# Three small copies on ScalarE in each of 24 dense units, and nine wide matmuls instead of twelve at the start

## The chip, the core and the metric

The kernel runs on one core of a Trainium2 chip. A core has five engines that run side by side, each with a list of instructions of its own: TensorE (PE in the profile, its weight loads PEld), VectorE (DVE), ScalarE (ACT), GpSimd (POOL) and SyncE (SP, which only issues transfers here). The metric is the device time of one execution in microseconds; the figure for the kernel before is a median of 3 runs.

## The reference

Three computations that share no data, in float32:

```
# 1 retention attention, 2 x 8 heads, 768 steps, width 64
for t in range(S):
    state = gamma * state + k[t] (x) v[t]          # 64 x 64 a head
    y[t] = scale * q[t] @ state
# 2 dense feed-forward, 1536 tokens, 512 -> 2048 -> 512
h = x @ w_in
out = maximum(0.01 * h, h) @ w_out
# 3 feed-forward with 8 experts, 512 -> 1024 -> 512
logits = x @ w_gate
e = argmax(logits); gate = softmax(logits)[e]
out[i] = gate[i] * (relu(x[i] @ w1[e]) @ w2[e])    # up to 384 tokens an expert
```

In this kernel they are chained: the attention's output is the input of the dense part, and that of the dense part the input of the experts.

## The kernel before

Weights and activations of the large matmuls are split into a high and a low part of reduced width, and each product is made as three (high x high, low x high, high x low); ScalarE makes a high part with one copy, VectorE the low part with one subtraction.

**The front.** The sequence runs as 12 chunks of 128 steps (named 0 to 9, a, b). The constant `LOADS` sets the order in which SP issues the loads (q0, k0, q1, w00 ...), and the constant `FRONT` sets the order of all steps of attention and of the first dense units, on all engines: `S.0` scores of chunk 0 (L190, PE), `am` the mask that multiplies them (L212, DVE), `M` scores times values (L256, PE), `ks` scaled keys (L198, DVE for the first two chunks, L202, ACT for the others), `D` the state's update (L228, PE), `Y` queries times state (L245, PE), and so on. Ahead of `S.0` PE runs matmuls on a tile of zeros whose results nobody reads: twelve wide ones (L1023, 512 columns) and one that clears the state (L217, `zero_state`); after `S.0` it runs 24 narrow ones (L1075, 64 columns), while VectorE makes the first masks.

**The dense part** is 64 units. A unit is 12 matmuls into `ps_h` (L363), then ScalarE copies them (`hs`, L370), VectorE applies the leaky maximum (L375), ScalarE rounds to the high part (`gh`, L379), VectorE makes the low part (`gl`, L385), and two units later (`LAG = 2`) PE multiplies by the second weight (L414, `ps_y`). Twelve units are begun in the front (the variable `reached` counts them, so it is 12), the loop that the diff touches runs over the others, i = 12 to 63. The function `slot()` in it puts the conversion of further weights between the steps (L297, L308 on ScalarE, L291 and others on VectorE).

**The experts** are 8, each with 8 units of weights. How many tokens an expert has is known only when the kernel runs, so the code of each is there three times, for 2, for 3 and for 1 tile of 128 tokens, in this order, and a comparison on every engine (L1231, L1232) jumps to the body that is run:

```
with tc.If(n > base + P, preferred_fallthrough_block=True, label=f"many{s}") as many:
    with tc.If(n <= base + 2 * P, preferred_fallthrough_block=True) as two:
        expert(s, 2, o)
    with two.Else():
        expert(s, 3, o)
with many.Else():
    expert(s, 1, o)
```

With this input the experts s = 0 to 7 run the bodies for 2, 3, 1, 1, 1, 1, 2 and 2 tiles. In a body, `mm_h` (L820 for one tile, L826 for two and three) makes h, `gh` (L868, ACT) and `gl` (L869, DVE) split it, `mm_y` (L878) makes y, and `og` (L982 on ACT, L980 on DVE) scales it by the gate. In the body for one tile all 8 h come first and then all 8 y. `conv_next` converts one unit of weights, ScalarE the high part `hi` (L848) and VectorE the low part `lo` (L849); behind an expert's own weights it takes up the first three units of the next expert, in the full width of 1024. It may do so only when the y whose buffer it takes has been made, so in a body for one tile these three stand behind the last `gh`, while PE is at the 8 y. The lines L747 and L750 are the comparisons of `by_class`, which choose between three ways to transpose the next expert's tokens, and L1302 a hint to the branch at the next expert.

## Time and profile before

| | |
|---|---|
| median of 3 runs | 533.26 us (532.6 to 534.32) |
| the profiled execution's own time | 533.35 us |
| its span in the trace | 531.6 us |
| mean granted clock of TensorE | 0.994 |
| busy share PE / PEld / DVE / ACT / POOL | 96% / 86% / 64% / 45% / 10% |

The span runs from the first to the last recorded work; the 1.75 us by which the execution's own time is longer lie around it. Busy shares are shares of the span. In the rows below, a line of a timeline gives the start, the time that the group took, the engine, the line of the program, the operation, what it writes and reads, how many there are, and in brackets how long the engine was idle just before and what ended that.

### The profile page before, as it was taken

What the parts mean: (1) busy time and instruction counts of PE and PEld (TensorE: products, weight loads), DVE (VectorE), ACT (ScalarE), POOL (GpSimd) and SP (SyncE); (2) the same over time, 40 slices, a digit from 0 to 9 for tenths busy, and PEclk for the clock granted to TensorE, in tenths of its full rate; (3) what the DMA queues carried; (4) which work ended last, traced back from release to release, by engine and by line L of the source; (5) the groups of instructions that cost most, each with busy time, mean ns of one, the idle gap of its engine ahead of it and who ended that gap; (6) DMA issues with size and microseconds to landing.
All of it is one profiled execution on the core that took longest, in us unless ns stands there. A gap on an engine that the chain in (4) does not pass through costs nothing.

```text
span 531.6 us, 8978 instructions
## 1 busy us (share of the span) xinstructions
PE 511.9 (96%) x3330; PEld 458.4 (86%) x3330; DVE 338.7 (64%) x670; ACT 241.0 (45%) x501; POOL 51.9 (10%) x75
## 2 busy tenths in 40 slices
PE   8899999999999999999999999999699989999994
PEld 5888989989998899988999998889599978889893
DVE  3999994379779748954733365667444445676560
ACT  1886963354344424432431314256243455556440
POOL 0000000000000000000100027242100211220101
PEclk9999999999999999999999999999989999999999
DMA  8987672022325602220210108599263298992001
GB/s 319 369 269 260 224 251 94 1 81 79 100 53 175 222 7 80 80 80 0 80 59 2 60 10 326 171 301 328 90 229 103 67 360 301 350 344 79 23 10 43
DMA packets 24939, 80.79 MB, mean 152 GB/s; under 512 B 3706, under 2 KB 3834, under 8 KB 24864
## 3 DMA queue, kind: packets, MB, share of 16 engines
q1 hardware_dynamic: 21312, 70.26, 37.8%
q0 software_dynamic: 3552, 9.58, 5.1%
q8 instruction: 40, 0.66, 0.5%
q14 instruction: 35, 0.29, 0.2%
HBM read 72.35 MB, written 9.96 MB: 155 GB/s over the span
## 4 chain that ended last, share of the span: by engine, by line
PE 72%; DMA 21%; DVE 3%; issue 1%; ACT 1%; POOL 0%; POOLq 0%; ACTq 0%; DVEq 0%
PE ps_h L363 24%; PE ps_y L414 16%; DMA out<-og,gix 12%; DMA xr<-x2d,gix 7%; PE ps_a L414 7%; PE ps_y L878 5%; PE ps_h L826 5%; PE ps_a L256 2%; PE ps_a L190 2%; PE ps_a L245 2%; PE ps_a L463 1%; PE ps_h L704 1%; DMA xpre<-wc,wix 1%; PE ps_y L715 1%; PE ps_y L1023 1%
## 5 line engine op out<-in xcount | busy, mean ns | idle before, releaser
L370 ACT ACTIVATE hs<-ps_h 128x384 f32<-128x384 f32 x64 | 31.5, 492 | 108.6 <-PE ps_h L363 108.6
L375 DVE SCALAR_TENSOR_TENSOR hs<-hs 128x384 f32<-128x384 f32 x64 | 35.6, 556 | 65.8 <-ACT hs L370 65.6
L414 PE MATMUL ps_y<-hi,gh 128*128 128x512 f32 x138 | 56.3, 408 | 0.0
L363 PE MATMUL ps_h<-xh,hi 128*128 128x384 f32 x256 | 55.8, 340 | 0.0
L363 PE MATMUL ps_h<-xh,lo 128*128 128x384 f32 x256 | 54.9, 336 | 0.0
L363 PE MATMUL ps_h<-xl,hi 128*128 128x384 f32 x256 | 54.8, 336 | 0.0
L414 PE MATMUL ps_y<-hi,gl 128*128 128x512 f32 x138 | 54.5, 395 | 0.0
L414 PE MATMUL ps_y<-lo,gh 128*128 128x512 f32 x138 | 54.4, 394 | 0.0
L379 ACT ACTIVATE gh<-hs 128x384 fp32r<-128x384 f32 x64 | 33.7, 526 | 43.5 <-DVE hs L375 43.5
L363 PEld LDWEIGHTS ps_h<-xh,hi 128*128 128x128 f32 x256 | 45.9, 188 | 5.3
L385 DVE TENSOR_TENSOR gl<-hs,gh 128x384 fp32r<-128x384 f32 x64 | 35.6, 557 | 21.3 <-ACT gh L379 21.3
L363 PEld LDWEIGHTS ps_h<-xl,hi 128*128 128x128 f32 x256 | 45.3, 188 | 0.0
L363 PEld LDWEIGHTS ps_h<-xh,lo 128*128 128x128 f32 x256 | 45.3, 188 | 0.0
L849 DVE TENSOR_TENSOR lo<-xland,hi 128x1024 fp32r<-128x1024 f32 (+1 forms) x32 | 33.6, 1056 | 14.0 <-ACT hi L848 13.4
L878 PE MATMUL ps_y<-hi,gh 128*128 128x512 f32 x104 | 41.2, 396 | 0.0
L878 PE MATMUL ps_y<-hi,gl 128*128 128x512 f32 x104 | 41.0, 394 | 0.0
L878 PE MATMUL ps_y<-lo,gh 128*128 128x512 f32 x104 | 40.8, 392 | 0.0
L849 DVE TENSOR_TENSOR lo<-land,hi 128x1024 fp32r<-128x1024 f32 (+1 forms) x30 | 31.2, 1044 | 10.3 <-ACT hi L848 9.9
L869 DVE SCALAR_TENSOR_TENSOR gl<-ps_h,gh 128x256 fp32r<-128x256 f32 (+2 forms) x42 | 16.6, 395 | 26.0 <-ACT gh L868 25.7
L848 ACT ACTIVATE hi<-xland 128x1024 fp32r<-128x1024 f32 (+1 forms) x32 | 29.2, 920 | 7.4 <-PE ps_y L878 7.4
L868 ACT ACTIVATE gh<-ps_h 128x256 fp32r<-128x256 f32 (+2 forms) x42 | 15.3, 363 | 38.0 <-PE ps_h L826 23.9
L414 PEld LDWEIGHTS ps_y<-hi,gl 128*128 128x128 f32 x138 | 25.9, 188 | 5.8
(200 smaller groups left out, 1000.0 us busy)
## 6 DMA issues: line engine op xcount, KB each, us to landing
land<-wc SPq DMA_DIRECT2D x32, 512.0 KB, 6.7
xland<-wc SPq DMA_DIRECT2D x32, 512.0 KB, 5.0
land<-wb SPq DMA_DIRECT2D x31, 512.0 KB, 4.9
land<-qkv SPq DMA_DIRECT2D x19, 512.0 KB, 5.4
out<-zero SPq DMA_DIRECT2D x12, 256.0 KB, 6.3
x2d<-rows SPq DMA_DIRECT2D x12, 256.0 KB, 2.1
early<-qkv SPq DMA_DIRECT2D x5, 512.0 KB, 7.0
cst<-cst_in SPq DMA_DIRECT2D x1, 512.0 KB, 5.5
```

The source lines that it names most:

```text
L363: nc.tensor.matmul(out=h_ps, lhsT=w[i][:, dc * P:(dc + 1) * P], rhs=x[j][:, dc, :], start=(n == 0), stop=(n == 3 * KD - 1))
L370: nc.scalar.activation(out=hs, in_=gt[u][0], func=ACTF.Copy)
L375: nc.vector.scalar_tensor_tensor(out=hs, in0=hs, scalar=0.01, in1=hs, op0=ALU.mult, op1=ALU.max)
L379: nc.scalar.activation(out=gh, in_=gt[u][0], func=ACTF.Copy)
L385: nc.vector.tensor_tensor(out=gl, in0=hs, in1=gh.bitcast(F32), op=ALU.subtract)
L414: nc.tensor.matmul(out=yb[ti][t], lhsT=gt[u][i][:, t * P:(t + 1) * P], rhs=w[j][:, 512:1024], start=(f == fs[0] and n == 0), stop=(f == fs ...
L826: r = nc.tensor.matmul(out=hp, lhsT=w[i][:, dc * P:(dc + 1) * P], rhs=(h, l)[j][:, dc, 0:cls * P], start=(n == 0), stop=(n == 3 * KD - 1))
L848: nc.scalar.activation(out=hi[:, o], in_=src[:, o], func=ACTF.Copy)
L849: nc.vector.tensor_tensor(out=lo[:, o], in0=src[:, o], in1=hi[:, o].bitcast(F32), op=ALU.subtract)
L868: nc.scalar.activation(out=gh, in_=hp, func=ACTF.Relu)
L869: nc.vector.scalar_tensor_tensor(out=gl, in0=hp, scalar=0.0, in1=gh.bitcast(F32), op0=ALU.max, op1=ALU.subtract)
L878: nc.tensor.matmul(out=yps[t], lhsT=gg[i][:, t * P:(t + 1) * P], rhs=w[j][:, 512:1024], start=(k == 0 and n == 0), stop=(k == PF - 1 and n ...
```

## The change

It has three parts. On TensorE three of the twelve wide matmuls on zeros go, and three narrow ones are added. On ScalarE each of the 24 units i = 12 to 35 of the dense loop gets three copies of one number into a tile `tick` that nothing reads. No other line is changed.

```diff
         nc.scalar.activation(out=bias_e, in_=zero[:, 0:1], func=ACTF.Copy)
+        tick = sm_p.tile([1, 1], F32, name="tick", bufs=1)
         wm = bank("y2", [P, DM])
-        for i in range(12):
+        for i in range(9):
             nc.tensor.matmul(out=wm, lhsT=zb[:, 0:P], rhs=zb[:, 0:DM], start=True, stop=True)
         zero_state(0)
...
             if n == "S" and c[0] == 0:
-                for _ in range(24):
+                for _ in range(27):
                     nc.tensor.matmul(out=wm[0:32, 0:64], lhsT=zb[:, 0:32], rhs=zb[:, 0:64], start=True, stop=True)
...
             slot()
             if i == len(units) - 1:
                 break
+            if i - reached < 24:
+                for _ in range(3):
+                    nc.scalar.activation(out=tick, in_=zero[0:1, 0:1], func=ACTF.Copy)
             u = units[i - LAG]
             ensure(u[1], 1)
```

On TensorE at the start of the program, before the change, the last wide matmuls on the tile `zero`, the state's clearing, the scores and the first narrow matmuls stand like this (a LDWEIGHTS row loads the weights of the matmul under it):

```order
L1023 LDWEIGHTS zero
L1023 MATMUL ps_y<-zero 128x512
L217 LDWEIGHTS zero
L217 MATMUL ps_h<-zero 128x512
L190 MATMUL ps_a<-early 128x128 x8
L1075 LDWEIGHTS zero
L1075 MATMUL ps_y<-zero 32x64
```

And with the change (the line numbers grow by one):

```order
L1024 LDWEIGHTS zero
L1024 MATMUL ps_y<-zero 128x512
L217 LDWEIGHTS zero
L217 MATMUL ps_h<-zero 128x512
L190 MATMUL ps_a<-early 128x128 x8
L1076 LDWEIGHTS zero
L1076 MATMUL ps_y<-zero 32x64
```

The order is the same; ahead of the first piece nine pairs stand instead of twelve, so everything from L217 on is six instructions earlier, and behind the narrow ones the counts are equal again.

On ScalarE in the dense loop, before the change, one unit follows the other like this (`hs` and `gh` are a unit's copies, `cv_a` and `hi` the conversion of a further weight, `rows` a finished output):

```order
L424 ACTIVATE rows<-ps_y 128x512 x3
L370 ACTIVATE hs<-ps_h 128x384
L379 ACTIVATE gh<-hs 128x384
L297 ACTIVATE cv_a<-cv_a,bias_e 128x512 x2
L370 ACTIVATE hs<-ps_h 128x384
L379 ACTIVATE gh<-hs 128x384
L308 ACTIVATE hi<-cv_a 128x512 x2
```

And with the change, over the same units:

```order
L424 ACTIVATE rows<-ps_y 128x512 x3
L370 ACTIVATE hs<-ps_h 128x384
L379 ACTIVATE gh<-hs 128x384
L297 ACTIVATE cv_a<-cv_a,bias_e 128x512 x2
L1144 ACTIVATE tick<-zero 1x1 x3
L370 ACTIVATE hs<-ps_h 128x384
L379 ACTIVATE gh<-hs 128x384
L308 ACTIVATE hi<-cv_a 128x512 x2
L1144 ACTIVATE tick<-zero 1x1 x3
```

The three copies stand in front of the next unit's `hs`, behind `gh` or behind the conversion of a weight; nothing else changes places.

On ScalarE at the end of the body for one tile of expert s = 2, before the change, after the comparisons about the transposes, stand the last `gh`, the three conversions for the next expert, the scaled output and the jump out of the body:

```order
L785 ACTIVATE cxf<-ps_a 128x256
L750 UNCONDITIONAL_BRANCH
L868 ACTIVATE gh<-ps_y 128x128
L848 ACTIVATE hi<-xland 128x1024
L747 UNCONDITIONAL_BRANCH
L848 ACTIVATE hi<-xland 128x1024 x2
L982 ACTIVATE og<-ps_y,tab 128x512
L1231 UNCONDITIONAL_BRANCH
```

And with the change:

```order
L785 ACTIVATE cxf<-ps_a 128x256
L750 UNCONDITIONAL_BRANCH
L868 ACTIVATE gh<-ps_y 128x128
L848 ACTIVATE hi<-xland 128x1024
L747 UNCONDITIONAL_BRANCH
L848 ACTIVATE hi<-xland 128x1024 x2
L982 ACTIVATE og<-ps_y,tab 128x512
L1235 UNCONDITIONAL_BRANCH
```

The rows are the same but for the line number. What moves is their place in ScalarE's list: 72 instructions are added ahead of them, and 26 semaphore instructions fall away there (the built program has 372 on ScalarE before and 346 with the change), because a wait that had an instruction of its own now rides on a copy. So every body of an expert on ScalarE stands 46 instructions later. The lists of the other engines keep their length and order, but for the three matmuls above.

## Rows read from the trace of the kernel before

**Rows 1.** The page, part 1: TensorE's busy time, share of the span, instructions.

```profile
PE 511.9 (96%) x3330; PEld 458.4 (86%) x3330; DVE 338.7 (64%) x670; ACT 241.0 (45%) x501; POOL 51.9 (10%) x75
```

**Rows 2.** The chain of waits, 355 to 532 us: who waited for whom, total, times, longest.

```profile
PE ps_y L820 <- DVE lo L849: 2.7, 3, 1.1
...
PE ps_h L820 <- DVE lo L849: 1.1, 1, 1.1
```

**Rows 3.** Timeline of TensorE, ScalarE and VectorE, end of s = 2 and start of s = 3.

```profile
428.09 0.48 PE L878 MATMUL ps_y<-hi,gh 128*128 128x512 f32 x1
...
433.70 1.05 PE L820 MATMUL ps_h<-cxf,xland 128*128 128x128 f32 x8
435.83 1.16 PE L820 MATMUL ps_h<-cxf,xland 128*128 128x128 f32 x8 [1.08 <-DVE lo L849]
438.11 2.05 PE L820 MATMUL ps_y<-cxf,xland 128*128 128x128 f32 x16 [1.11 <-DVE lo L849]
...
428.60 0.27 ACT L868 ACTIVATE gh<-ps_y 128x128 fp32r<-128x128 f32 x1
433.46 2.95 ACT L848 ACTIVATE hi<-xland 128x1024 fp32r<-128x1024 f32 x3 [4.60 <-PE ps_y L878]
...
434.56 3.50 DVE L849 TENSOR_TENSOR lo<-xland,hi 128x1024 fp32r<-128x1024 f32 x3 [5.14 <-ACT hi L848]
437.97 0.29 DVE L869 SCALAR_TENSOR_TENSOR gl<-ps_h,gh 128x128 fp32r<-128x128 f32 x1
```

**Rows 4.** Timeline of ScalarE, the same place in s = 3, 4 and 5.

```profile
448.97 2.00 ACT L848 ACTIVATE hi<-land 128x1024 fp32r<-128x1024 f32 x2 [3.01 <-PE ps_y L878]
...
462.87 2.01 ACT L848 ACTIVATE hi<-xland 128x1024 fp32r<-128x1024 f32 x2 [2.52 <-PE ps_y L878]
...
478.95 1.06 ACT L848 ACTIVATE hi<-land 128x1024 fp32r<-128x1024 f32 x1 [3.33 <-PE ps_h L826]
```

**Rows 5.** The transfers of 431 to 433.6 us: instruction fetches (packets, MB, share).

```profile
q14 instruction: 1, 0.01, 0.7%
```

**Rows 6.** Timeline of TensorE and VectorE, the start of the program.

```profile
1.19 5.30 PE L1023 MATMUL ps_y<-zero 128*128 128x512 bf16 x12 [1.19 <-DVE zero L1019]
6.28 0.63 PE L217 MATMUL ps_h<-zero 128*128 128x512 bf16 x1
6.84 1.16 PE L190 MATMUL ps_a<-early 64*128 64x128 f32 x16
7.94 0.87 PE L1075 MATMUL ps_y<-zero 128*32 128x64 bf16 x24
...
9.38 0.98 PE L256 MATMUL ps_a<-am,early 128*64 128x128 f32 x13 [0.17 <-DVE am L212]
...
8.04 1.29 DVE L212 TENSOR_TENSOR am<-ps_a,cst 128x512 f32<-128x512 f32 x2 [6.91 <-PE ps_a L190]
```

**Rows 7.** Timeline of SP: the loads that it issues, each behind an earlier landing.

```profile
5.31 1.66 SPq L164 DMA_DIRECT2D land<-qkv  x2
...
8.69 0.33 SPq L164 DMA_DIRECT2D land<-qkv  x1
```

**Rows 8.** Windows: busy time of each engine, PEclk (granted clock), DMA share, GB/s.

```profile
385.00:389.10 4.10, 4.04 (x14) 4.07 (x15) 0.00 (x0) 0.30 (x1) 0.00 (x0) 0.58 0.02 6
```

**Rows 9.** ScalarE: the smallest copy, `hs` in 100 to 200 us (busy, mean | idle), and one tight unit.

```profile
2.03 0.20 ACT L1020 ACTIVATE bias_e<-zero 128x1 f32<-128x1 f32 x1
...
L370 ACT ACTIVATE hs<-ps_h 128x384 f32<-128x384 f32 x24 | 11.8, 491 | 38.4 <-PE ps_h L363 38.4
...
121.82 0.49 ACT L370 ACTIVATE hs<-ps_h 128x384 f32<-128x384 f32 x1 [0.71 <-PE ps_h L363]
```

**Rows 10.** Timeline of ScalarE, VectorE and TensorE in the body of s = 1.

```profile
410.68 1.05 ACT L848 ACTIVATE hi<-land 128x1024 fp32r<-128x1024 f32 x1
...
415.02 0.56 DVE L869 SCALAR_TENSOR_TENSOR gl<-ps_h,gh 128x384 fp32r<-128x384 f32 x1 [2.03 <-ACT gh L868]
...
418.48 0.39 PE L878 MATMUL ps_y<-hi,gh 128*128 128x512 f32 x1
```

## The prediction, made before the changed kernel ran

> **What bounds the kernel now.** I read the page first: TensorE is busy 96% of the span [rows 1], so time can only be won where it stands idle, or where its matmuls run at the lower clock. The chain of waits, then, for the experts: what ends TensorE's idle time there, beside one branch, is VectorE's `lo`, 2.7 us in three pieces and 1.1 us in one [rows 2], 3.8 us in all. In the dense part TensorE's timeline shows no idle stretch. So three places matter: those four pieces, the start, and the dense units for the cover that they give.

> [...]

> **The change part by part.**

> *Bodies 46 places later.* The copies add 72 instructions ahead of the experts and 26 semaphore instructions go. Borders then lie 46 places earlier in the code than now. I followed each through the bodies that this input runs: the four in the bodies for one tile fall into code for three tiles, which isn't run there, and one enters run code, in s = 1. Without a stop the first conversion of s = 2 starts at about 429.05. The first `lo` started 1.10 us after its conversion (434.56 less 433.46), and the three took 3.50: they end at 429.05 + 1.10 + 3.50 = 433.65. TensorE wants them after its first eight matmuls of s = 3, at 433.70 + 1.05 = 434.75. So they are 1.1 us early, and so, by the same shape, in the other three. The four pieces go whole: minus 3.8 us. What is late next is nothing on these rows: TensorE itself.

> *The border in s = 1.* It falls beside the conversion at 410.68, ahead of the last `gh` [rows 10]. With the longest stop seen, the conversion starts at 415.3 and ends at 416.3, `gh` takes some 0.5 and its `gl` starts near 416.9, ending at 417.5 (0.56 us). TensorE reads that at 418.48. So about 1 us of cover is left; a stop over 5.6 us would show. Bound 0 to 0.3; I take 0.1.

> *Nine wide matmuls.* Twelve and what follows start 6.28 - 1.19 = 5.09 us apart, 0.424 each, so three are 1.27 us [rows 6]. The scores could start at 6.84 - 1.27 = 5.57; SP's row at 5.31, which stands behind the landing of the first load, says that their data is there by then [rows 7]. [...] The 16 scores of 128 columns, 6.84 to 7.94, are 0.069 apart, a quarter of 0.234 and a little: full pace. [...] Gain 0.65. [...] Behind the scores the mask follows 0.04 us on [rows 6], and everything in `FRONT` hangs on that chain. The scaled keys need a constant that lands at 8.67 (SP goes on at 8.69, [rows 7]) and wouldn't start 0.65 earlier than their 9.24, but 0.55; `D`, which wants them, follows the M matmuls at about 9.55, and the keys end near 9.4. I take 0.65 of 0 to 1.27.

> *Three more narrow matmuls.* 0.87 / 24 is 0.036 each, so 0.11 us, ahead of M; M waits 0.17 us for the second mask two matmuls later (9.38), which takes it up [rows 6]. Cost 0; without that cover 0.11.

> *The 72 copies.* The smallest copy in the rows, 128 by 1, takes 0.20 us; three make 0.6 us a unit. They stand ahead of `hs`, where ScalarE idles for TensorE's h anyway: 38.4 us over 24 units between 100 and 200 us, 1.6 us each [rows 9]. A tight unit has 0.71. Where the cover fails `hs` is later by some tenths, and behind it VectorE's leaky maximum, `gh` and `gl`; TensorE reads them two units on, four blocks of matmuls of about 2 us, against a chain of some 3.5. So 0; uncovered everywhere it would be 24 x 0.6 = 14 us. Lower bound 0: nothing waits for the copies.

> **The sum.** 533.35 (the profiled execution) - 3.8 - 0.65 + 0.1 = 529.0. That execution lies 0.09 above the median of the runs, so the sum holds for a median as well. Its own range: from 533.35 - 3.8 - 1.27 = 528.3, less 0.4 for runs, to 530.3, where the start gives nothing and a fifth of the stops stays: 527.9 to 530.3.

> **The rivals.**

> 1. *The start gives nothing or costs.* After the branch into s = 1 the rows show a stretch of 4.1 us at a granted clock of 0.58 behind TensorE's idle time [rows 8]: low pace can last some us. [...] Chance 0.12.

> 2. *The stops move instead of going.* The jumps into the bodies for one tile now lead from one block into the next, which they don't today on ScalarE. If such a jump misses, `gh` at the start of the next expert is late and the conversions behind it with it. VectorE makes a jump of this kind between s = 2 and s = 3 now, and its row at 437.97 shows no idle time behind the `lo` before it [rows 3], which speaks against. With half to all of the 3.8 given back: 530.9 to 532.7. Chance 0.16, about half of it under the 531.7 that can be told from no change. [...]

> 3. *A border costs nothing,* the regular distance is an accident, and `lo` stays late for a transfer or for y. Then only the start counts: 532.7. Against it: the wandering place. Chance 0.06.

> 4. *Slower: the copies stand in TensorE's way.* In the dense units, ScalarE's `hs`. The lag of two units hides one delay, not one that adds up: with an idle 1.6 us a unit [rows 9] three copies decide once each costs over 0.53 us (they write one tile, so each may wait for the last); each 0.1 us more costs 24 x 0.3 = 7.2 us. At 0.75 us each, 24 x 0.66 = 16 us are lost and 545 is the result. For it: no row has a copy that writes what the last one wrote. Against it: 0.20 us for 128 numbers. Chance 0.06.

> My forecast keeps 0.60. About 0.3%, 1.6 us, can be told from no change here: faster is under 531.7, which holds for the forecast, rival 1 and half of rival 2, 0.80; same is the other half and rival 3, 0.14; slower is rival 4, 0.06. The range takes the forecast, rival 1 and two thirds of rival 2, some 0.82: 527.9 to 532.2.

> **What would show it.** In the chain of waits of the changed kernel TensorE's four waits for `lo` are gone, and ScalarE's conversions in s = 2 to 5 start within 0.5 us of their y, with no idle time over 2 us. In s = 1 ScalarE idles once for 3 to 5 us near 410 us, and TensorE doesn't. The first mask starts at about 7.4, not 8.04. The copies show as 72 rows of some 0.2 us, with `hs` at its old distance from h. Wrong would be: new idle time on TensorE at the start of s = 3 to 6 behind `gh`; the same four waits; a gap ahead of L414 between 100 and 200 us; scores that end at 8.0.

## The result and the profile after

The kernel with the change took 527.14 us in the median of 4 runs (526.82 to 529.48), the kernel before 533.33 us beside it: a ratio of 0.9892, with an interval of 0.986 to 0.9925. A further comparison of the same two kernels (below) gave 0.987 [0.9835, 0.9904]. The profiled execution took 526.96 us, its span 525.1 us, 6.5 less than before. The prediction was 529.0 with a range from 527.9: the direction was right, the gain was 6.2 us and not 4.3, and the time lies under the range.

In the chain of waits, 355 to 526 us, no row has TensorE wait for `lo` any more; what is left of [rows 2] is VectorE's own wait, 12.2 us in 25 pieces, none over 1.2, and the branch into s = 1:

```profile
DVE lo L849 <- ACT hi L848: 12.2, 25, 1.2
...
PE ps_h L826 <- issue: 4.2, 1, 4.2
```

The timeline at the place of [rows 3], end of s = 2 and start of s = 3, ScalarE, VectorE, then TensorE:

```profile
427.88 0.27 ACT L868 ACTIVATE gh<-ps_y 128x128 fp32r<-128x128 f32 x1
428.45 2.96 ACT L848 ACTIVATE hi<-xland 128x1024 fp32r<-128x1024 f32 x3 [0.30 <-PE ps_y L878]
433.28 0.69 ACT L982 ACTIVATE og<-ps_y,tab 128x512 f32<-128x512 f32 x1 [1.87 <-PE ps_y L878]
434.31 0.28 ACT L868 ACTIVATE gh<-ps_h 128x128 fp32r<-128x128 f32 x1 [0.34 <-PE ps_h L820]
...
429.54 3.50 DVE L849 TENSOR_TENSOR lo<-xland,hi 128x1024 fp32r<-128x1024 f32 x3 [0.84 <-ACT hi L848]
...
433.08 1.95 PE L820 MATMUL ps_h<-cxf,xland 128*128 128x128 f32 x16
434.86 1.39 PE L820 MATMUL ps_y<-cxf,xland 128*128 128x128 f32 x11
```

The conversions start after 0.30 us of idle time, not 4.60, and `lo` ends at 433.04, before TensorE has begun s = 3. There is no idle time in TensorE's rows. The same three conversions stand together without a stop in s = 3, 4 and 5. Windows show the stretch as a whole: 427 to 467 us (TensorE, PEld, VectorE, ScalarE, GpSimd, then granted clock, DMA share, GB/s), first of the kernel with the change:

```profile
427.00:467.00 40.00, 40.00 (x285) 36.96 (x284) 27.15 (x52) 26.46 (x56) 7.41 (x8) 1.00 0.96 356
```

and of the kernel before:

```profile
427.00:467.00 40.00, 36.27 (x241) 32.46 (x241) 23.11 (x42) 22.75 (x47) 8.38 (x7) 1.00 0.90 328
```

TensorE was busy 36.27 of 40 us and is now busy all of them, and 285 matmuls are done there in place of 241. The start, as in [rows 6]:

```profile
1.19 4.02 PE L1024 MATMUL ps_y<-zero 128*128 128x512 bf16 x9 [1.19 <-DVE zero L1019]
5.00 0.63 PE L217 MATMUL ps_h<-zero 128*128 128x512 bf16 x1
5.56 1.55 PE L190 MATMUL ps_a<-early 64*128 64x128 f32 x16
7.04 0.96 PE L1076 MATMUL ps_y<-zero 128*32 128x64 bf16 x27
8.18 1.40 PE L256 MATMUL ps_a<-am,early 128*64 128x128 f32 x16 [0.18 <-DMA early<-qkv]
...
7.15 1.29 DVE L212 TENSOR_TENSOR am<-ps_a,cst 128x512 f32<-128x512 f32 x2 [6.02 <-PE ps_a L190]
8.89 0.69 DVE L198 TENSOR_TENSOR ks<-early,cst 128x512 f32<-128x512 f32 x1 [0.45 <-DMA cst<-cst_in]
```

The first mask starts 0.89 us earlier (8.04 to 7.15). Ahead of M, TensorE now waits 0.18 us for a load (k0), and the scaled keys wait 0.45 us for their constant. In `early30` the scores start at 5.28 and not at 5.56, and `D` (L228), after 0.33 us of waiting for the keys, at 9.58 where it was 9.63: earlier scores alone gain next to nothing there.

And the copies, all in one group, with the `hs` behind them (groups of ScalarE, 100 to 200 us):

```profile
L1144 ACT ACTIVATE tick<-zero 1x1 f32<-1x1 f32 x72 | 14.2, 197 | 1.5
...
L370 ACT ACTIVATE hs<-ps_h 128x384 f32<-128x384 f32 x24 | 11.7, 489 | 26.9 <-PE ps_h L363 26.9
```

They take 14.2 us of ScalarE, and its idle time ahead of `hs` falls from 38.4 [rows 9] to 26.9 us: most of the copies' time lies in it.

**Where the 6.5 us of span came from.** I followed the same matmuls through both traces, by the starts of their rows:

| place | before | after | gained up to there |
|---|---|---|---|
| second chunk's `Y` (L245) | 17.90 | 17.04 | 0.86 |
| routing (L505) | 330.22 | 328.97 | 1.25 |
| s = 1, first h | 385.06 | 383.95 | 1.11 |
| s = 3, first h | 433.70 | 433.08 | 0.62 |
| s = 5, the row that had waited last | 466.38 | 461.05 | 5.33 |
| second output's transfer of s = 7 | 525.61 | 519.43 | 6.18 |

The four pieces are worth 4.71 us (5.33 - 0.62), the start 0.86, and 0.85 comes after the fourth stop. About 0.5 us is lost again after the branch into s = 1, where the granted clock over the first 8 us is 0.70 and was 0.79 before (windows from the first h on).

These are the figures of one pair of executions, and what the stops cost differs between executions. From the first h of s = 3 to the second output's transfer of s = 7 the trace before has 91.91 us and the trace after 86.35. Of the further kernels below, those with four stops have 89.97 (`nine_only`), 90.10 (`back128`) and 90.45 (`late_refill`), those without a stop there 86.14 to 86.75. So the stops are worth 3.6 to 5.6 us, and the trace before is at the upper end. (`six_wide`, 92.48, has a mean granted clock of 0.96 from 420 to 468 us, where it was 1.00 before and in `nine_only`, and is left out; see below.)

### The profile page after: what moved, and what is told of

Same layout as the page of the kernel before. It is cut to its first block, busy times and chain, and to the rows that moved or that the text cites. A ratio compares the mean times of both kernels' runs of the same rounds, so it can differ in the third digit from the quotient of the medians.

```text
span 525.1 us, 9022 instructions
## 1 busy us (share of the span) xinstructions
PE 509.6 (97%) x3328; PEld 459.9 (88%) x3330; DVE 338.7 (64%) x670; ACT 253.2 (48%) x573; POOL 50.1 (10%) x75
## 3 DMA queue, kind: packets, MB, share of 16 engines
q1 hardware_dynamic: 21312, 70.26, 38.4%
q0 software_dynamic: 3552, 9.58, 5.2%
## 4 chain that ended last, share of the span: by engine, by line
PE 68%; DMA 24%; DVE 3%; issue 2%; ACT 1%; POOL 0%; SPq 0%; POOLq 0%; ACTq 0%; DVEq 0%
PE ps_h L363 25%; PE ps_y L414 16%; DMA out<-og,gix 12%; DMA xr<-x2d,gix 8%; PE ps_a L414 7%; PE ps_h L826 5%; PE ps_y L878 5%; PE ps_a L256 2%; PE ps_a L190 2%; PE ps_a L245 1%; DMA xpre<-wc,wix 1%; DMA early<-qkv 1%; PE ps_a L463 1%; DMA land<-qkv 1%; PE ps_h L228 1%
## 5 line engine op out<-in xcount | busy, mean ns | idle before, releaser
L414 PE MATMUL ps_y<-hi,gh 128*128 128x512 f32 x138 | 56.3, 408 | 0.0
L414 PE MATMUL ps_y<-hi,gl 128*128 128x512 f32 x138 | 53.9, 391 | 0.0
L414 PE MATMUL ps_y<-lo,gh 128*128 128x512 f32 x138 | 53.8, 390 | 0.0
L414 PEld LDWEIGHTS ps_y<-hi,gl 128*128 128x128 f32 x138 | 25.9, 188 | 5.6
L414 PEld LDWEIGHTS ps_y<-hi,gh 128*128 128x128 f32 x138 | 25.9, 188 | 4.1 <-issue 0.3
```

Source lines behind the costliest of these rows:

```text
L414: nc.tensor.matmul(out=yb[ti][t], lhsT=gt[u][i][:, t * P:(t + 1) * P], rhs=w[j][:, 512:1024], start=(f == fs[0] and n == 0), stop=(f == fs ...
```

## The experiments

Twelve kernels ran, each with five rounds beside the kernel before on the same chip. The kernel before had medians of 533.3 to 535.2 us in these comparisons, a spread as large as some parts of the change, so ratios to the kernel before are compared. One cause of the spread shows in the traces: in some executions the granted clock drops between 330 and 350 us (0.83 in the profile of `nine_only`, 1.00 in the profiles before and after).

| kernel | ratio | 95% interval |
|---|---|---|
| the change, first comparison | 0.9892 | 0.986 to 0.9925 |
| `change_again` | 0.987 | 0.9835 to 0.9904 |
| `ticks_only` | 0.9892 | 0.9854 to 0.9931 |
| `nine_only` | 0.9973 | 0.9948 to 0.9998 |
| `back128` | 0.9965 | 0.9937 to 0.9992 |
| `early30` | 0.9891 | 0.9855 to 0.9927 |
| `more174` | 0.9901 | 0.9869 to 0.9933 |
| `six_wide` | 1.0013 | 0.9981 to 1.0045 |
| `late_hint` | 0.9974 | 0.994 to 1.0008 |
| `late_nine` | 0.9983 | 0.9948 to 1.0017 |
| `no_hint` | 0.9921 | 0.9893 to 0.9949 |
| `late_refill` | 1.0013 | 0.999 to 1.0036 |
| `hintless` | 0.9907 | 0.9874 to 0.9939 |

My theory after the result was the prediction's: a border between blocks of 128 instructions stops ScalarE (theory B). Its rivals were that the earlier start changes how things meet in the experts, that the copies gain in another way, and, once I saw that s = 1 has a border without a stop (below), that the branch hint is part of the cause (theory H).

**The two parts apart, `ticks_only` and `nine_only`.**

```diff
 # ticks_only: the copies alone
-        for i in range(9):
+        for i in range(12):
...
-                for _ in range(27):
+                for _ in range(24):
```

> The 72 copies alone, with twelve wide matmuls and 24 narrow ones as before. The trace after the change puts 4.7 us of the gain on the four places at the start of s = 3 to 6, counted from start to start of TensorE's matmuls, and 0.9 on the start. Border theory (the copies gain by moving code): 533.3 - 4.7 to 5.4, so 527.9 to 528.6. Rival (the earlier start changes how transfers and conversions meet in the experts, and the copies do nothing): 533.3, with ScalarE's four stops back.

```diff
 # nine_only: the matmuls alone
-            if i - reached < 24:
-                for _ in range(3):
-                    nc.scalar.activation(out=tick, in_=zero[0:1, 0:1], func=ACTF.Copy)
```

> Nine wide and 27 narrow matmuls alone, no copies: ScalarE's list is that of before. Border theory: ScalarE stops in s = 2 to 5 as before, for 2.5 to 4.6 us, and the time is 533.3 - 0.9 = 532.4. Rival (the start is the cause in the experts too): no stops, 527 to 528.

The copies alone have the ratio of the whole change, 0.9892. The matmuls alone bring 0.27% (0.02 to 0.52), 1.4 us and not well known. ScalarE's stops are there in `nine_only`, 3.61 us in s = 2, 2.29, 2.35 and 3.27 behind it, and `ticks_only` has none: its conversions there wait 0.89 us at most. So the start is not the cause of what happens in the experts.

**The same borders with more copies, `back128`, and the change's borders with more, `more174`.**

```diff
-                for _ in range(3):
+                for _ in range(6 if i - reached < 14 else 7):   # back128
```

> The change with 154 copies in place of 72 (six in each of 14 units, seven in each of ten), so that every expert's body on ScalarE stands exactly 128 instructions later than before the change: the borders between blocks of 128 fall on the same instructions as before it. Border theory: the four stops are back at the same rows, ahead of the first, the second, the second and the third conversion, and the time is 532.4. Rival (copies, by their number or by what they do to the dense part, are what gains): 527 or less. If copies cost time, 6.4 a unit at 0.2 us would show ahead of the dense units' matmuls.

```diff
-                for _ in range(3):
+                for _ in range(8 if i - reached < 16 else 9):   # more174
```

> The change with 200 copies in place of 72 (eight in each of 16 units, nine in each of eight): the bodies stand 174 instructions later, which is 46 and 128, so the borders fall where the change has them. Both theories: no stops, and if the copies stay hidden the time of the change, 527.1. If they cost (rival 4 of the prediction): 8.3 copies a unit at 0.2 us are 1.7 us, just what ScalarE idles ahead of hs; where they push hs behind by more than the lag of two units covers, a gap ahead of the dense part's second matmuls, up to 24 x 0.4 = 10 us, 537.

In `back128` the stops are back, in the same rows as in [rows 3] and [rows 4]: with three, two, two and one conversion left (timeline of ScalarE):

```profile
434.82 2.95 ACT L848 ACTIVATE hi<-xland 128x1024 fp32r<-128x1024 f32 x3 [3.74 <-PE ps_y L878]
...
449.48 2.00 ACT L848 ACTIVATE hi<-land 128x1024 fp32r<-128x1024 f32 x2 [2.15 <-PE ps_y L878]
...
463.56 2.00 ACT L848 ACTIVATE hi<-xland 128x1024 fp32r<-128x1024 f32 x2 [2.71 <-PE ps_y L878]
...
479.48 1.06 ACT L848 ACTIVATE hi<-land 128x1024 fp32r<-128x1024 f32 x1 [3.17 <-PE ps_h L826]
```

Its ratio, 0.9965, is near that of the nine wide matmuls alone, 0.9973. With 46 and 128 more, `more174`, the gain is there. That settles that the place in the list, taken modulo 128, decides, and not the copies.

With each stop goes a fetch of instructions: inside each of the four before, a block of 8 KB (q14, 0.31 us long) starts 1.4 to 1.7 us before the conversion does, at 432.00 (the one of [rows 5]), 447.58, 461.41 and 477.29. Of the four stops 3.1, 1.6, 1.1 and 1.7 us lie ahead of the block. Whose instructions it holds the transfers don't say.

`more174` also answers the fourth rival: 200 copies leave ScalarE 3.2 us of idle time ahead of `hs` in the 24 units (26.9 with 72), and TensorE has no gap there. Groups of ScalarE, 99 to 199 us (196 of the copies fall into it):

```profile
L1144 ACT ACTIVATE tick<-zero 1x1 f32<-1x1 f32 x196 | 39.2, 200 | 5.6
...
L370 ACT ACTIVATE hs<-ps_h 128x384 f32<-128x384 f32 x24 | 11.2, 465 | 3.2 <-PE ps_h L363 3.2
```

**A border in the run bodies, but ahead of the hint, `early30`.** Theory B doesn't explain s = 1 after the change. There the border lies between the last `gh` but one and the conversion behind it, in code that is run, and the timeline of ScalarE after the change shows the two rows without a gap:

```profile
409.78 0.49 ACT L868 ACTIVATE gh<-ps_h 128x384 fp32r<-128x384 f32 x1 [2.72 <-PE ps_h L826]
410.17 1.06 ACT L848 ACTIVATE hi<-land 128x1024 fp32r<-128x1024 f32 x1
```

What set the four stops apart from it is the branch hint (L1302): in a body for one tile it stands fourteen instructions in, ahead of the border, in that for three tiles behind it.

```diff
-            if i - reached < 24:
+            if i - reached < 16:
```

> The change with 48 copies (three in each of 16 units): bodies stand 30 instructions later, and in s = 2 to 5 the border falls near the start of the run body, about six instructions in, ahead of the branch hint for the next expert, which stands 14 in. Theory B (any border in these bodies stops ScalarE): a stop of 3 to 5 us near the third gh of each of these experts; what comes behind it is late by up to that much, some of it covered, so 528 to 532. Theory H (a border stops ScalarE only when it stands behind the body's branch hint, which turns the fetching of instructions to the hinted place): no stop over 1 us that TensorE doesn't explain, and 527.2.

The ratio is that of the change, and at the borders of s = 3, 4 and 5 nothing stops. In s = 3 the border lies behind the second conversion of these rows, ahead of the third `gh` (timeline of ScalarE):

```profile
436.52 0.28 ACT L868 ACTIVATE gh<-ps_h 128x128 fp32r<-128x128 f32 x1 [0.34 <-PE ps_h L820]
436.69 0.62 ACT L848 ACTIVATE hi<-xland 128x512 fp32r<-128x512 f32 x1
437.32 0.28 ACT L868 ACTIVATE gh<-ps_h 128x128 fp32r<-128x128 f32 x1
437.50 0.62 ACT L848 ACTIVATE hi<-xland 128x512 fp32r<-128x512 f32 x1
438.21 0.28 ACT L868 ACTIVATE gh<-ps_y 128x128 fp32r<-128x128 f32 x1
```

So theory B falls: a border alone costs nothing here, with no idle time at these rows. One stop was there that neither theory had named: in s = 2, ahead of the first `gh` and before the border, ScalarE stands 2.67 us up to 424.77. It makes s = 2 about 1 us longer (14.08 us to the first h of s = 3, 13.11 after the change).

**The hint moved behind the border, `late_hint` and `late_nine`.**

```diff
 # both start from the kernel before, without copies
             if i == NAME[cls] and not last:
-                name_next(s + 1)
+                name_next(s + 1, ENGS[:1] + ENGS[2:3] if cls == 1 else ENGS[:3])
+            if i == 11 and cls == 1 and not last:
+                name_next(s + 1, ENGS[1:2])
 # late_nine: range(9) wide and range(27) narrow besides
```

> The kernel before the change, no copies, twelve wide matmuls; one edit: in the bodies for one tile, ScalarE's branch hint stands behind the three conversions for the next expert and not behind the fourth gh (TensorE's and VectorE's stay where they were). ScalarE's list has the same length, and the borders between blocks of 128 stay where they were, two instructions on in the code of these bodies, still between the last gh and the scaled output. Theory B (a border behind a jump stops ScalarE): the four stops stay, 533. Theory H (the border stops it because the hint has turned the fetching to the hinted place): the border is now ahead of the hint, the stops in s = 2 to 4 go, and in s = 5 too or nearly so; 533.3 - 4.7 = 528.6.

> The same edit to the hint with nine wide and 27 narrow matmuls, no copies. Theory H: both gains without a copy, 533.3 - 4.7 - 0.9 = 527.7, the time of the change within 0.3%. Theory B: the start alone, 532.4.

Three of the four stops are gone, with the borders where they were; the one in s = 2 stays (timeline of ScalarE in `late_hint`, s = 2, 3 and 5):

```profile
436.45 2.00 ACT L848 ACTIVATE hi<-xland 128x1024 fp32r<-128x1024 f32 x2 [4.14 <-PE ps_h L820]
446.77 2.96 ACT L848 ACTIVATE hi<-land 128x1024 fp32r<-128x1024 f32 x3 [0.44 <-PE ps_y L878]
...
473.41 2.96 ACT L848 ACTIVATE hi<-land 128x1024 fp32r<-128x1024 f32 x3
```

It makes TensorE wait 2.14 us at 439.96, about as much in one piece as the two in [rows 3]. Both times missed what I had expected: 0.9974 and 0.9983, with intervals that reach 1. In the trace of `late_hint` the stretch from the first h of s = 3 to the last transfer of s = 7 takes 89.18 us, 2.7 less than before and 0.8 to 1.3 less than in the other traces with four stops; a gain of this size the ratios can't show. In that of `late_nine` (90.56 us) 16 matmuls of L820, from 439.91 on, take 3.5 us and not 1.78.

**The hints taken out, `no_hint`.**

```diff
 # from the kernel before; five copies in the first dense unit besides, for the place of the borders
-        for e in (mybir.EngineType.PE, mybir.EngineType.Activation, mybir.EngineType.DVE):
+        for e in (mybir.EngineType.PE, mybir.EngineType.DVE):
             tc.mark_branch_hint_location(f"many{s}", hint=over(s, e, 1), engines=[e])
+        for _ in range(2):
+            nc.scalar.activation(out=tick, in_=zero[0:1, 0:1], func=ACTF.Copy)
```

> The kernel before the change with ScalarE's branch hints taken out: in every body two of the one-number copies stand in place of the hint and the instruction ahead of it, and five copies in the first dense unit keep the borders at the places of before (ahead of the first, the second, the second conversion, and in s = 5 at the scaled output); TensorE's and VectorE's hints stay. Theory H in full (the hint, that of the body before too, is what keeps the next block from being fetched in time): no stops in s = 2 to 4; the four waits of TensorE go, 528.6, less what the jumps cost without a hint, up to about 1 us each where ScalarE has no slack. Theory J (a body that was entered by a jump into another block has its next block fetched only at the border, hint or not): the stop in s = 2 stays at 3 to 5 us, as it did with the late hint, and those in s = 3 and 4 depend on how their blocks were entered: across a border, so they go.

With the borders at the places of before, and transfers 98% busy there, no conversion stops, in s = 2 neither (timeline of ScalarE):

```profile
432.46 0.28 ACT L869 ACTIVATE gh<-ps_y 128x128 fp32r<-128x128 f32 x1
433.17 2.96 ACT L849 ACTIVATE hi<-xland 128x1024 fp32r<-128x1024 f32 x3 [0.43 <-PE ps_y L879]
...
446.27 2.96 ACT L849 ACTIVATE hi<-land 128x1024 fp32r<-128x1024 f32 x3 [0.42 <-PE ps_y L879]
```

The ratio is 0.9921. Theory J falls: without a hint no conversion idles over 0.43 us at a border, where it was 2.52 to 4.60 us before. So a hint is part of the cause; that it acts through the fetching is my guess, which no trace shows. Where it stands in the same body ahead of the border, theory H holds in every trace. For s = 2 of `late_hint` it doesn't: no hint of its own body stands ahead of that border, the nearest is that of s = 1, and ScalarE stopped; `no_hint` hasn't that one either, and it didn't. But a hint of the body before is not enough for a stop. One runs ahead of the border in s = 3 to 5 of `late_hint` and of `early30` too, and in s = 1 after the change, and nothing stops there. What is special about s = 2 is not shown.

**Loads at another time, `late_refill`.**

```diff
-            refills(i)
+            if cls > 1:
+                refills(i)
```

> The kernel before the change with one edit: in the bodies for one tile SP issues the loads of further weights at the end of the expert and not unit by unit, so that few or none are under way while ScalarE comes to the border in s = 2 to 5. ScalarE's list is unchanged. Theory D (the next block's fetch is issued in time but lies queued behind weight loads, the transfers being 86% busy there): the stops shrink to under 2 us and TensorE's waits for lo with them, 529 to 530, unless late loads make TensorE wait. Theory H: the stops stay at 2.5 to 4.6 us, 533.

The stops stayed (3.77, 1.98, 2.94 and 3.22 us), as did the time. But the edit didn't do what I meant: transfers were 98% busy between 427 and 440 us with it, so it doesn't tell what a stop lasts in a quiet stretch. That a busy queue alone makes the stop is refuted by `no_hint`, which is as busy there.

**Twelve to six, `six_wide`.**

```diff
-        for i in range(12):
+        for i in range(6):
...
-                for _ in range(24):
+                for _ in range(30):
```

> Six wide and 30 narrow matmuls, no copies: the step from twelve to nine doubled. The first load lands at 5.29, so the scores can't start before 5.3, against 5.56 with nine, and TensorE idles from about 3.7 to 5.3. If the granted clock rises by the time alone, as the pace of the scores suggests (at about 7.05 with twelve, 6.45 with nine), the scores end near 7.0 as with nine, 532.4. If it needs TensorE busy ahead of it, the rise comes later, the scores and masks run at half pace, and the time is back at 533.3 or above.

By the pace the second of the two outcomes; for the clock that it speaks of, the window of 0 to 20 us gives 1.00. Timeline of TensorE at the start:

```profile
3.72 0.63 PE L217 MATMUL ps_h<-zero 128*128 128x512 bf16 x1
5.21 2.08 PE L190 MATMUL ps_a<-early 64*128 64x128 f32 x16 [0.85 <-DMA early<-qkv]
7.21 1.78 PE L1075 MATMUL ps_y<-zero 128*32 128x64 bf16 x30
8.92 1.10 PE L256 MATMUL ps_a<-am,early 128*64 128x128 f32 x16
```

TensorE idles 0.85 us ahead of the scores, and all 16 of them and the narrow matmuls run at a slower pace (2.08 us for 16, where they took 1.16 before; 1.78 for 30, where 27 take 0.96 after the change): M starts at 8.92 and not at 8.18. The ratio, 1.0013, shows no gain.

**Without hints and without copies, `hintless`, and the change again.**

```diff
 # hintless: nine wide and 27 narrow matmuls, no copies, and
-        for e in (mybir.EngineType.PE, mybir.EngineType.Activation, mybir.EngineType.DVE):
+        for e in (mybir.EngineType.PE, mybir.EngineType.DVE):
```

> Nine wide and 27 narrow matmuls, no copies, and ScalarE's branch hints simply left out (TensorE's and VectorE's stay). The bodies move by up to 42 instructions to the front. If the hints are what makes the borders cost, the time of the change without a copy: no ScalarE stops in s = 2 to 5, 533.3 - 4.7 - 0.9 = 527.7, within 0.3% of the change beside it. If ScalarE needs the hint at its jumps, a wait of 1 to 3 us ahead of the first gh of each expert, some of it on TensorE's path: 529 to 533.

> The change itself once more, unaltered, on the same chip as the kernel without hints: 0.986 to 0.9925 of the kernel before, by its first four runs; with more runs nearer to 0.989.

0.9907 [0.9874, 0.9939] beside 0.987 [0.9835, 0.9904] on the same chip. The intervals overlap; the kernel without hints is not shown to be slower than the change, and not better either. No stop and no wait ahead of a first `gh` shows in it. So the hints on ScalarE gain nothing that I could find, and no version here beats the change. What a border costs without a hint this kernel doesn't tell: by the count of its instructions, the borders at these places fall into the bodies for two tiles in s = 2 to 5, which aren't run there. The test of a border without a hint is `no_hint`.

## Why the prediction was right in direction and wrong in size

**The stops.** That they belong to the border, and go whole, was right: [rows 3] and [rows 4] showed a stop that wanders through equal code, and `back128` brings it back by 128 places. The step that failed is the first term of the sum, *bodies 46 places later*: 3.8 us, and measured 4.71 in this pair of traces, with 0.85 more behind it. The 3.8 is a sum of idle times in the rows, and an idle time runs from the modelled end of the matmul before. TensorE's matmuls overlap: eight of L820 take 1.05 us by their row, but 16 follow the next group after 1.78 (433.08 to 434.86 above), so eight hold TensorE for 0.89. Start to start, the wait at 435.83 in [rows 3] is 435.83 - 433.70 - 0.89 = 1.24 us and not 1.08, that at 438.11 is 438.11 - 435.83 - 0.89 = 1.39 and not 1.11. Two pieces of four are 0.44 us larger. The other two, in s = 4 and 5, are 452.48 - 449.50 - 1.78 = 1.20 us and not 1.03, and 466.38 - 463.92 - 1.78 = 0.68 and not 0.51 (timeline of TensorE before):

```profile
449.50 1.95 PE L820 MATMUL ps_h<-cxf,land 128*128 128x128 f32 x16
452.48 2.05 PE L820 MATMUL ps_y<-cxf,land 128*128 128x128 f32 x16 [1.03 <-DVE lo L849]
...
463.92 1.95 PE L820 MATMUL ps_h<-cxf,xland 128*128 128x128 f32 x16
466.38 2.05 PE L820 MATMUL ps_y<-cxf,xland 128*128 128x128 f32 x16 [0.51 <-DVE lo L849]
```

That makes 4.51. The rest of the 4.71 lies in the groups behind the waits at 438.11 and 452.48, which hold TensorE for 1.88 and 1.89 us, where 1.78 is usual.

Part of the miss is which execution was profiled: by the other traces the stops, the fourth included, are worth 3.6 to 4.1 us, near the 3.8, and only the trace before has 5.6. One cost of the stops was in no term. In two of the seven traces whose conversions stop in s = 2 TensorE is slower behind its wait for `lo`: 16 matmuls that else follow each other in 1.78 us take 3.5 and 3.4. The mean granted clock of these executions is 0.987 and 0.982, where `late_hint` has 0.991 (timeline of TensorE, `late_nine`, then `six_wide`):

```profile
439.91 3.68 PE L820 MATMUL ps_y<-cxf,xland 128*128 128x128 f32 x16 [1.90 <-DVE lo L849]
...
442.69 3.56 PE L820 MATMUL ps_y<-cxf,xland 128*128 128x128 f32 x16 [1.11 <-DVE lo L849]
```

No timeline of TensorE without that stop has such a group there (after, `early30`, `more174`, `no_hint`, `hintless`, `change_again`). By the medians the copies alone gain 5.8 us (`ticks_only`), more than most pairs of traces show; that these slow groups make up the difference is not shown.

**The fourth stop.** Priced at nothing, as no wait on TensorE in [rows 2] follows it. The table above shows 0.85 us gained after 466.38, where only that stop was left. 0.10 of it is the group behind the third wait, and about 0.55 comes in s = 6 between 478 and 485 us: there TensorE's weight loads wait for a `lo` (timeline of the weight loads before), and the matmul groups around it follow each other more slowly than after the change.

```profile
483.12 0.54 PEld L826 LDWEIGHTS ps_h<-cxh,lo 128*128 128x128 f32 x4 [0.24 <-DVE lo L849]
```

[rows 2] show TensorE's matmuls, and there such a wait has no row. What makes the neighbouring groups slower is not shown.

**The border in s = 1.** 0.1 us was taken for a stop that isn't there. The premise, that every border in run code stops ScalarE, is the one that the experiments refuted.

**The start.** 0.65 predicted, 0.86 measured in this pair. The term was an estimate of what the clock does at the start, and no run shows it: the windows give a granted clock of 1.00 from 1 to 10 us before and after, but the trace's record of it begins only at 6.81 us before and at 6.41 after. What the rows show is the pace. The 16 scores take 1.16 us before and 2.08 in `six_wide`, 1.8 times as long; after the change they take 1.55, so some of them ran at the faster pace. The moment at which the pace changes isn't fixed to the number of wide matmuls either: in the trace of `ticks_only`, with twelve, the scores start at 6.44, not at 6.84, and the matmul ahead of them (L217) takes 0.38 us, not 0.63. So the size of this term is in part luck. The second chunk's `Y` starts at 17.90, 17.87, 17.57, 17.50 and 16.93 in the five traces with twelve wide matmuls (before, `late_refill`, `late_hint`, `ticks_only`, `no_hint`) and between 16.96 and 17.27 in the eight with nine: the means lie 0.46 us apart, and this pair of traces is near the largest difference. `nine_only` by its times says 0.02% to 0.52%.

**The rivals.** The first (the start gives nothing or costs) was wrong for nine wide matmuls; six gave nothing that shows. The second (the stops move to the jumps) is refuted: `og` at 433.28 and the first `gh` of s = 3 at 434.31 lie close together, with 0.34 us of idle time that TensorE's row explains. In another layout it does happen: the 2.67 us of `early30` stand behind the jump into s = 2. The third is refuted by `back128`, the fourth by `more174`; 0.197 us each was the predicted 0.20.

**The range.** Its low end took the start's upper bound and 0.4 us for runs, but held the first term at 3.8 as if it were exact. With both ends for that term, 3.8 to 4.7, it would have reached 527.0 and held the time. The miss is small beside the noise: 529.0 is 0.9919 of the time before, which the first interval (0.986 to 0.9925) holds and the second (0.9835 to 0.9904) doesn't.

**What stays open.** What a hint does, so that ScalarE stands at a border; whether the block of 8 KB inside each stop is the next of its list; why s = 2 of `late_hint` stops behind a hint of the body before and the borders in s = 3 to 5 don't; why s = 2 in `early30` stands 2.67 us ahead of its first `gh`; how long the stop would be with quiet transfers; and the 4.1 us of TensorE at the branch into s = 1, which none of the kernels touched.

## What to carry to other kernels

A wait whose named releaser has long been done, and which turns up at a different row in each repetition of the same code, is worth a count of the instructions in the list: equal distances of 128 here named the cause that no row of ScalarE's timeline names. Move the code by a few instructions as a test, then back by the whole period: the second run separates the place from the instructions that were added. Where an engine's branch hints stand a few instructions ahead of such a border, try the kernel without the hints, and hold the borders in place while you do: left out, they move the code, and the borders may fall elsewhere, as in `hintless`. And a wait of TensorE is priced from start to start of its matmuls, not by the idle time of its rows, which is short by 0.16 to 0.28 us a piece here. Last, what a stop costs is read from several executions: one pair of traces gave 5.6 us here, where others give 3.6 to 4.1.

## What the runs showed of the hardware that was not expected

- At a border between blocks of 128 instructions ScalarE idled 0.43 us at most in `no_hint`, 0.98 at most in s = 3 to 5 of `late_hint`, and not at all in s = 1 after the change and in s = 3 to 5 of `early30`. Where the branch hint of the same body ran ahead of it, ScalarE stood 1.98 to 4.60 us at every one (four each before and in `nine_only`, `back128` and `late_refill`). In s = 2 of `late_hint` and `late_nine` it stood 4.14 and 3.90 us with no hint ahead of the border but those of bodies before.
- The granted clock of TensorE between 330 and 350 us was 1.00 in ten of the fourteen executions profiled, 0.83 in three (`nine_only`, `six_wide`, `no_hint`) and 0.91 in `back128`, with the same instructions there. From the routing's first matmul (L505, the row of the table) to the first h of s = 2 `six_wide` took 95.61 us, the kernels before and after the change 90.37 and 91.00; not all of that need be this drop, as the clock behind the branch into s = 1 differs too (0.66 to 0.83 from 383 to 393 us). Differences of this size exceed the start's part, so a single time of this kernel can't show it.
- Two hundred copies of one number, 0.2 us each, in the dense part cost nothing measurable, eight or nine in a unit: the ratio is 0.9901 (`more174`), where 72 copies have 0.9892.
